# Linear attention into a gated MLP on one core: the first w_in chunk in three loads, batch 2's queries transposed by TensorE, and two block products left whole

## The chip, the cores and the metric

The kernel runs on one core of one Trainium2 chip. The metric is the device time of one execution in microseconds, lower is better. The core has five engines with instruction streams of their own: TensorE (PE in the profile, its weight loads PEld), VectorE (DVE), ScalarE (ACT), GpSimd (POOL) and SyncE (SP). They run side by side and wait for each other through semaphores. SP, ACT and POOL also start DMA transfers.

## The reference

Eight batches of eight heads with 576 rows of 64 values go through an attention without a score matrix; its output, 4608 rows of 512 values, goes through a layer of 2048 units with the activation h * sigmoid(beta * h).

```python
q_s = exp(q - max(q, -1));  q_s = q_s / (sum(q_s, -1) + 1e-09)     # softmax over the 64 values of a row
k_s = exp(k - max(k, 2));   k_s = k_s / (sum(k_s, 2) + 1e-09)      # softmax over the 576 rows
kv  = einsum('bhsd,bhse->bhde', k_s, v)
x   = einsum('bhsd,bhde->bhse', q_s, kv)       # to rows of 512: 8 heads x 64
h   = x @ w_in                                 # 4608 x 512 @ 512 x 2048
g   = h * (1.0 / (1.0 + exp(-beta * h)))
out = g @ w_out                                # 2048 x 512
```

All inputs and the output are float32.

## The kernel before

**Slabs.** The 4608 rows are cut into nine slabs `t` of 512 rows: slabs 0 to 7 are the first 512 rows of batches 0 to 7, slab 8 holds the last 64 rows of all eight batches. A slab has two passes on PE. Pass 1 makes the hidden units: 16 tiles of 128 units, each of four matmuls of 512 columns over the four 128-row blocks `m` of w_in (`pass1_lead` for the first three tiles, block by block; `pass1_tile` for the others; L377). ACT puts each tile through Silu into GT (L623), DVE divides it by beta (L646).

**Pass 2.** From slab 1 on (`pass2_fast`, L712) the second pass forms the product with w_out by seven block products in place of eight, in the manner of Strassen and Winograd: each product is 8 steps `i` of two matmuls of 256 columns, 16 matmuls, 112 in all (L723). Sums of blocks of GT are made by DVE for them: GS1 and GS2 (`g_sum1` L677, `g_sum2` L682, made in parts as the tiles come, the last part for step 7 after the last tile), and the differences `g_diff(0)` and `g_diff(1)` (L689) in place. Sums of blocks of w_out (WSUM, L701) are made once, in slab 0. The first product goes into bank `s`, the second into bank `z5`, the third into `z2`. DVE copies `s` to TS (L792), subtracts `z5` (L795), later `z2` (L801). Before the change the first two products are interleaved: steps 0 to 5 of the first, steps 0 to 5 of the second, steps 6 and 7 of the first, steps 6 and 7 of the second.

**Attention, mixed in.** The attention of batch t + 1 is done while slab t runs. ACT takes exponentials of q and k (EQ, EK; L300). `norm_main` (L324) normalizes EQ for `n` head pairs: a row sum on DVE (L331), a reciprocal on DVE (QI, L332), and a multiplication in place on DVE or POOL as its last argument says (L333). The normalized queries must be transposed to QT, in one of two ways: `t_steps` (L379) has PE transpose four 128x128 blocks for each head pair into a PSUM bank (L375) and ACT or DVE copy them out (L395); `turn` (L480) has the DMA crossbar do it, issued by SP (L484). `norm_turn` is `norm_main` on POOL for two head pairs, followed by `turn`. `kv_steps` (L425) multiplies k and v on PE, with two head pairs to a bank, then a reciprocal (L439) and two masked scalings to KVD (L419) on DVE. `out_step` (L451) is one matmul of 512 columns, KVD with QT, and a copy to XT (L457), which is what pass 1 of the next slab reads.

**The order.** Each engine works through its instructions in the order in which the program adds them. PE's order is set by slots: in each slab, pass 1 takes slots 0 to 64 and pass 2 slots 64 to 128. Each matmul of pass 1 advances the count by 1, each of the 112 of pass 2 by 32/56. A list `todo` of (slot, step) pairs is worked off as the count passes them; `spread(steps, lo, hi)` places steps evenly between two slots. `attn_late(b)` (L509) gives the list for batch b in slabs 1 to 3. Work of the other engines that goes with pass 2 is tied to hooks 0 to 7, points between the products: hook 0 before the first product, 1 and 2 around the first subtraction, 3 after the third product.

**Slab 0.** The loads of w_in and w_out are started by POOL in sequence (`load_win` L545, `load_wout` L551; they cast to bf16). w_in's first chunk of 512 units comes in two parts of two blocks `m` each, the three others whole. Batch 1's q is loaded when w_out's first chunk has landed (L901). Its four head pairs are then normalized one by one and transposed by PE in slots 97, 106, 114 and 119 of slab 0, whose second pass is plain (`pass2_group`, 64 matmuls of 512 columns). Between the normalizations DVE makes the rest of WSUM.

Of the kernel before, what the change touches and what calls it, by code (L numbers as in the profile page):

```python
# [20 lines left out]
NG = NF // 2  # L21
# [133 lines left out]
def bass_efficient_attn_shen__then__act_swish_beta_kernel(  # L155
# [12 lines left out]
    with ExitStack() as es:  # L168
# [340 lines left out]
        def attn_late(b):  # L509
            x = []  # L510
            for hp in range(NHP):
                x += out_step(b, hp, MB, ACTE if hp % 2 else DVE)
            k01, k23 = kv_steps(b, (0, 1)), kv_steps(b, (2, 3))
            if b < 4:
                s = spread(k01, 97, 101) + spread(k23, 101, 105) + [(105, lambda: g_diff(1))]
                return s + spread(x[0:2], 117, 120)
            s = spread(k01, 92, 96) + spread(k23, 96, 99.8) + [(100, lambda: g_diff(1))]
            return s + spread(x, 107, 123)
# [26 lines left out]
        def load_win(c0, c1, m0=0, m1=NM):  # L545
            a = bass.AP(win_h, c0 + 128 * m0 * DFF, [[DFF, 128], [128 * DFF, m1 - m0], [1, c1 - c0]])
            add(POOL, lambda e: e.dma_start(WIN[:, m0:m1, c0:c1], a),  # L547
                w=[("win", f, m) for f in range(c0 // 128, c1 // 128) for m in range(m0, m1)],
                slot=f"win{c0}_{m0}", after=P.writer[("kf", 0, 0)] if c0 == m0 == 0 else ())
# [21 lines left out]
        warm(10, 0)  # L571
        norm_main(0, 0, 1, DVE)
        norm_main(0, 1, 1, POOL)
        load_win(0, 512, 0, 2)
        load_win(0, 512, 2, 4)
        for c0 in range(512, DFF, 512):
            load_win(c0, c0 + 512)
# [134 lines left out]
        def pass2_fast(t, tick, hooks):  # L712
            s, z5, z2 = HB[hrot[0] % 3], OB[0], OB[1]
            z2s = (OB[1], MB[0]) if t == NSLAB - 1 else (z2, z2)

            def prod(bk, lhs, lk, rhs, rk, first, end=False, part=range(NG)):
                two = bk == z2 and z2s[0] != z2s[1]
                for i, u in ([(i, u) for u in range(2) for i in part] if two and end else
                             [(i, u) for i in part for u in range(2)]):
                    l, r_ = lhs(i, u), rhs(i)  # L720
                    st = first and i == 0 and (u == 0 or two)
                    b_ = z2s[u] if two else bk
                    add(PE, lambda e, l=l, r_=r_, st=st, u=u, i=i, b_=b_: e.matmul(  # L723
                        PS[b_][:, 256 * u:256 * u + 256], l, r_, start=st, stop=end and i == NG - 1,
                        skip_group_check=True),
                        r=lk(i) + rk(i), w=[("ps", b_)], bank=[b_])
                    tick(32.0 / 56)

            def gt(f0, th):
                return (lambda i, u: GT[:, f0 + i, 256 * th + 128 * u:256 * th + 128 * u + 128],  # L730
                        lambda i: [("gt", f0 + i, th)])

            def gs2(th):
                return (lambda i, u: GS2[:, i, 256 * th + 128 * u:256 * th + 128 * u + 128],
                        lambda i: [("gs2", i)])

            def wo(fh, dh):
                return (lambda i: WOUT[:, NG * fh + i, 256 * dh:256 * dh + 256],
                        lambda i: [("wout", NG * fh + i, dh)])

            def wsum(n):
                return lambda i: WSUM[n][:, i, :], lambda i: [("ws", n, i)]

            def out(th, dh):
                return (O2S[t % 2][:, 2 * th:2 * th + 2, 256 * dh:256 * dh + 256],
                        [("o2", t % 2, 2 * th + u, dh) for u in range(2)])

            def bank3(bk):
                return PS[bk][:, :].rearrange("p (a b) -> p a b", b=256)

            def halves(bk):
                if bk == z2 and z2s[0] != z2s[1]:
                    return [(z2s[0], 0, 1), (z2s[1], 1, 2)]
                return [(bk, 0, 2)]

            def copy(bk, th, dh, eng):
                o, w = out(th, dh)
                for b_, u0, u1 in halves(bk):
                    add(eng, lambda e, b_=b_, u0=u0, u1=u1: (  # L759
                        e.copy if eng == ACTE else e.tensor_copy)(  # L760
                        o[:, u0:u1, :], bank3(b_)[:, u0:u1, :]),
                        r=[("ps", b_)], w=w[u0:u1], bank=[b_])
                if t == 8:
                    store8(th, dh)

            def last(bk, th, dh):
                o, w = out(th, dh)
                ts = TS[:, :].rearrange("p (a b) -> p a b", b=256)
                h = halves(bk)
                for b_, u0, u1 in h:  # L770
                    add(DVE, lambda e, b_=b_, u0=u0, u1=u1: e.tensor_tensor(  # L771
                        o[:, u0:u1, :], ts[:, u0:u1, :], bank3(b_)[:, u0:u1, :], ALU.add),
                        r=["ts", ("ps", b_)], w=w[u0:u1], bank=[b_])
                    if t == 8 and len(h) == 2:
                        store8(th, dh, u0)
                if t == 8 and len(h) == 1:
                    store8(th, dh)

            def at(n):
                for f in hooks.get(n, ()):  # L780
                    f()

            at(0)
            def prod_s(part):
                prod(s, lambda i, u: GS1[:, i, 128 * u:128 * u + 128], lambda i: [("gs1", i)],
                     *wsum(0), True, True, part)

            prod_s(range(0, 6))
            prod(z5, *gs2(0), *wo(1, 1), True, False, range(0, 6))
            prod_s(range(6, NG))  # L790
            prod(z5, *gs2(0), *wo(1, 1), True, False, range(6, NG))
            add(DVE, lambda e: e.tensor_copy(TS[:, :], PS[s][:, :]), r=[("ps", s)], w=["ts"],  # L792
                bank=[s])
            at(1)
            add(DVE, lambda e: e.tensor_tensor(TS[:, :], TS[:, :], PS[z5][:, :], ALU.subtract),  # L795
                r=["ts", ("ps", z5)], w=["ts"], bank=[z5])
            at(2)
            prod(z2, *gs2(1), *wo(0, 0), True)
            for b_, u0, u1 in halves(z2):
                c = slice(256 * u0, 256 * u1)  # L800
                add(DVE, lambda e, b_=b_, c=c: e.tensor_tensor(  # L801
                    TS[:, c], TS[:, c], PS[b_][:, c], ALU.subtract),
                    r=["ts", ("ps", b_)], w=["ts"], bank=[b_])
            if t > 3:
                g_diff(0)
                g_diff(1)
            at(3)
            prod(z5, *gt(0, 0), *wo(0, 1), False)
            copy(z5, 0, 1, ACTE)
            at(4)  # L810
            prod(z2, *gt(NG, 1), *wo(1, 0), False)
            copy(z2, 1, 0, ACTE)
            at(5)
            prod(z5, *gt(0, 1), *wsum(1), False, True)
            last(z5, 1, 1)
            at(6)
            prod(z2, *gt(NG, 0), *wsum(2), False, True)
            last(z2, 0, 0)
            at(7)
# [12 lines left out]
        def one(fn, *a):  # L832
            return lambda: fn(*a)

        def steps(fn, *a):
            return lambda: go(fn(*a))

        for t in range(NSLAB):
# [12 lines left out]
                todo += [(2, steps(out_step, 0, 3, HEAD, DVE))]  # L851
            elif t < 4:
                todo = attn_late(t + 1)
                if t > 1:
                    todo += [(1, steps(out_step, t, 2, MB, ACTE)), (2.5, steps(out_step, t, 3))]
                if t == 3:
                    todo += [(4, one(norm_turn, 4, 2))]
                if t == 1:
                    todo += [(1, steps(out_step, 1, 2, (3,), ACTE)),
                             (3, steps(kv_steps, 1, (3,), (7,))),  # L860
                             (6, steps(out_step, 1, 3, (7,), DVE)),
                             (6.1, one(w_diff, 0)), (6.2, one(w_diff, 1))]
            elif t < 7:
                todo = attn(t + 1)
                if t > 3:
                    todo += spread(outr_steps(2 * t - 5), *((72, 88), (40, 56), (60, 76))[t - 4])
            elif t == 7:
                todo = spread(outr_steps(1), 32, 48)
# [31 lines left out]
            if t == 0:  # L900
# [6 lines left out]
                w_sum(0, 0, 4)  # L907
                w_sum(2, 0, 4)
                norm_main(1, 0, 1, DVE)
                norm_main(1, 1, 1, DVE)  # L910
                cast_vr_s(1)
                w_sum(0, 4, 4)
                w_sum(2, 4, 4)
# [29 lines left out]
            if t == 1:  # L943
                on(0, exps, 2)
                on(0, casts, 2)
                on(2, norm_turn, 2, 0)
                on(3, norm_turn, 2, 2)
                on(3, g_diff, 0)
                on(3, load, 4)
            elif t == 2:  # L950
                on(0, exps, 3)
                on(2, norm_turn, 3, 0)
# [67 lines left out]
```

## Time and profile before

| what | value |
|---|---|
| time, median of 3 runs | 274.92 us (274.59 to 274.92) |
| profiled execution, its own time | 274.92 us |
| its span | 273.1 us |
| granted clock of TensorE | 0.998 |
| PE, PEld busy | 265.5 us, 167.3 us |
| DVE, ACT, POOL busy | 193.3, 180.7, 62.2 us |
| slab 0: pass 1, pass 2 begin | 14.8, 28.9 us |
| slab 1: pass 1, pass 2 begin | 45.9, 61.1 us |
| slab 2: pass 1, pass 2 begin | 75.1, 89.4 us |
| slab 3: pass 1, pass 2 begin | 103.9, 117.9 us |
| slab 8: pass 2 begins | 257.1 us |

The span is the time from the first to the last instruction that the profile holds; the rest of the execution's own time lies around it. Times in the timeline are counted from the span's start. In a row of the timeline or of a group there stand the start and duration (or the total and mean), the engine, the line of the kernel, the operation, the tiles that it writes and reads with their shapes, and how often it occurs. "[0.63 <-DVE EQ L333]" says how long the engine was idle before, and which instruction released it. Matmul times are modelled: the records of two matmuls overlap, and the distance of their starts is what one takes.

### The profile page before, as it was taken

Reading aid. Unit: us, or ns where it says so; the run is one execution under the profiler, and the core shown is the slowest. Engines: PE = TensorE matmul, PEld = TensorE weight load, DVE = VectorE, ACT = ScalarE, POOL = GpSimd, SP = SyncE. Lnnn points to the kernel's source line nnn. Section 1 sums busy time; section 2 is a strip of 40 time slices with the busy share of each in tenths; the row PEclk is TensorE's granted clock in tenths of the full one; section 3 lists DMA queues with packets and bytes.
Section 4 is the critical chain, followed back from the end, with each engine's and each line's share of the span. In section 5 each row is a group of like instructions: output and inputs, shape, how many; then the busy total and the mean of one; then the engine's idle time right before and its main releaser. Section 6 shows DMA issues by size and latency. Waiting matters only on the chain.

```text
span 273.1 us, 4650 instructions
## 1 busy us (share of the span) xinstructions
PE 265.5 (97%) x1802; PEld 167.3 (61%) x1825; DVE 193.3 (71%) x415; ACT 180.7 (66%) x284; POOL 62.2 (23%) x81
## 2 busy tenths in 40 slices
PE   8899999999999999999999999999999999999994
PEld 2444445448844884478656875587558745874683
DVE  4954586787867799768776976977597549625762
ACT  4898558789287956896778847893783477018610
POOL 2780010006530099000910570037000100000000
PEclk9999999999999999999999999999999999999999
DMA  7999999989599239920499999103600130012005
GB/s 218 316 201 207 226 327 351 293 253 383 119 339 251 100 61 313 340 61 0 96 289 276 352 323 171 77 7 75 209 2 0 22 154 0 2 58 96 2 1 152
DMA packets 59365, 45.92 MB, mean 168 GB/s; under 512 B 28608, under 2 KB 58320, under 8 KB 58320
## 3 DMA queue, kind: packets, MB, share of 16 engines
q1 hardware_dynamic: 54480, 40.90, 52.7%
q0 software_dynamic: 4240, 4.19, 9.3%
q10 hardware_dynamic: 624, 0.53, 0.6%
q8 instruction: 14, 0.23, 0.3%
q14 instruction: 7, 0.06, 0.1%
HBM read 36.71 MB, written 9.44 MB: 169 GB/s over the span
## 4 chain that ended last, share of the span: by engine, by line
PE 80%; DMA 9%; DVE 4%; POOL 4%; issue 1%; ACT 0%; SPq 0%; POOLq 0%; DVEq 0%
PE PS L377 47%; PE PS L723 33%; DMA WOUT<-in_moe_w_out_dram 5%; DMA QF<-in_q_dram 3%; POOL EQ L333 2%; POOL WIN L547 1%; DVE QS L331 1%; DMA QT<-EQ 1%; DVE EQ L333 1%; DVE WSUM L701 0%; DVE QI L332 0%; PE PS L375 0%; DVE XT L457 0%; DVE TS L792 0%; DVE TS L795 0%
## 5 line engine op out<-in xcount | busy, mean ns | idle before, releaser
L377 PE MATMUL PS<-XT,WIN 128*128 128x512 bf16 x562 | 129.6, 379 | 0.8
L623 ACT ACTIVATE GT<-PS,BETA 128x512 bf16<-128x512 f32 x144 | 95.1, 689 | 38.8 <-PE PS L377 38.3
L377 PEld LDWEIGHTS PS<-XT,WIN 128*128 128x128 bf16 x576 | 53.7, 98 | 60.8 <-DVE XT L457 0.6
L646 DVE TENSOR_SCALAR GT<-GT,RB 128x512 bf16<-128x512 bf16 x144 | 51.7, 378 | 36.4 <-ACT GT L623 35.7
L333 POOL TENSOR_TENSOR EQ<-EQ,QI 128x1024 bf16<-128x1024 bf16 (+1 forms) x13 | 25.6, 1967 | 49.9 <-DVE QI L332 49.2
L723 PE MATMUL PS<-WOUT,GT 128*128 128x256 bf16 x256 | 33.9, 273 | 0.1
L723 PE MATMUL PS<-WOUT,GS 128*128 128x256 bf16 x256 | 31.8, 273 | 0.2
L723 PE MATMUL PS<-WSUM,GT 128*128 128x256 bf16 x256 | 30.4, 272 | 0.2
L723 PEld LDWEIGHTS PS<-WSUM,GT 128*128 128x128 bf16 x256 | 24.9, 98 | 4.0 <-issue 0.6
L723 PEld LDWEIGHTS PS<-WOUT,GT 128*128 128x128 bf16 x256 | 24.9, 98 | 3.4
L723 PEld LDWEIGHTS PS<-WOUT,GS 128*128 128x128 bf16 x256 | 24.5, 98 | 3.4
L759 ACT COPY O2S<-PS 128x512 f32<-128x512 f32 (+1 forms) x17 | 9.4, 560 | 25.6 <-PE PS L723 24.2
L300 ACT ACTIVATE EQ<-QF 128x512 bf16<-128x512 f32 x32 | 17.9, 619 | 7.8 <-DMA QF<-in_q_dram 7.7
L682 DVE TENSOR_TENSOR GS<-GT 128x512 bf16<-128x512 bf16 (+2 forms) x32 | 21.9, 685 | 0.0
L377 PE MATMUL PS<-VB,EK 128*128 128x129 bf16 x128 | 20.9, 220 | 0.2 <-DVE VB L348 0.2
L348 POOL CAST VB<-VF 128x512 bf16<-128x512 f32 x25 | 15.4, 617 | 24.1 <-DVE GS L682 14.5
L331 DVE TENSOR_REDUCE QS<-EQ 128x16 f32<-128x1024 bf16 (+1 forms) x20 | 19.8, 991 | 0.6 <-ACT EQ L300 0.6
L689 DVE TENSOR_TENSOR GT<-GT 128x2048 bf16<-128x2048 bf16 x16 | 20.1, 1283 | 0.0
L300 ACT ACTIVATE EK<-KF 128x512 bf16<-128x512 f32 x32 | 18.1, 620 | 0.0
L457 ACT CAST XT<-PS 128x512 bf16<-128x512 f32 x18 | 10.3, 581 | 10.6 <-PE PS L377 10.6
L771 DVE TENSOR_TENSOR O2S<-TS,PS 128x512 f32<-128x512 f32 (+1 forms) x17 | 10.7, 642 | 9.3 <-PE PS L723 9.3
L723 PE MATMUL PS<-WSUM,GS 128*128 128x256 bf16 x128 | 16.7, 273 | 0.0
(78 smaller groups left out, 232.3 us busy)
## 6 DMA issues: line engine op xcount, KB each, us to landing
out_dram<-O2S SPq DMA_DIRECT2D x8, 1024.0 KB, 5.2
QF<-in_q_dram SPq DMA_DIRECT2D x6, 1024.0 KB, 6.0
KF<-in_k_dram SPq DMA_DIRECT2D x6, 1024.0 KB, 8.5
VF<-in_v_dram SPq DMA_DIRECT2D x6, 1024.0 KB, 12.3
KF<-in_k_dram SPq DMA_DIRECT2D x8, 256.0 KB, 5.6
VF<-in_v_dram SPq DMA_DIRECT2D x8, 256.0 KB, 5.6
WOUT<-in_moe_w_out_dram POOLq DMA_DIRECT2D x4, 512.0 KB, 16.6
WIN<-in_moe_w_in_dram POOLq DMA_DIRECT2D x3, 512.0 KB, 9.2
```

Of the source, the lines that this page charges most:

```text
L300: add(ACTE, lambda e, o=o, a=a: e.activation(o, a, ACT.Exp), r=[(name + "f", i, hp)], w=[("e" + name, i, hp)])
L331: add(DVE, lambda e: e.tensor_reduce(s_, a, AX.X, ALU.add), r=ks, w=[("qs", i, hp0)])
L333: add(eng, lambda e: e.tensor_tensor(a, a, vb, ALU.mult), r=ks + [("qi", i, hp0)], w=ks)
L348: add(eng, lambda e: (e.copy if eng == ACTE else e.tensor_copy)(o, a), r=[("vf", i, hp), ("vone", i)], w=[("vb", i, hp)], after=after)
L377: add(PE, lambda e: e.matmul(o, l, r_, start=start, stop=stop), r=r, w=w, bank=[bk])
L457: add(eng, lambda e: (e.copy if eng == ACTE else e.tensor_copy)(XT[i][:, hp, :], PS[bk][:, :]), r=[("ps", bk)], w=[("xt", i, hp)], bank=[bk])
L623: add(ACTE, lambda e: e.activation(GT[:, f, :], PS[bk][:, :], ACT.Silu, scale=BETA[:, f:f + 1]), r=[("ps", bk), "beta"], w=[("gt", f, 0), ...
L646: add(DVE, lambda e: e.tensor_scalar(GT[:, f, :], GT[:, f, :], RB[:, f:f + 1], None, ALU.mult), r=k + ["rb"], w=k)
L682: add(DVE, lambda e: e.tensor_tensor(GS2[:, i:i + n, :], GT[:, i:i + n, :], GT[:, i + NG:i + NG + n, :], ALU.add), r=[k_ for f in (i, i + ...
L689: add(DVE, lambda e: e.tensor_tensor(gv(f, th, NG), gv(f, th, NG), gv(f, 1 - th, NG), ALU.subtract), r=gk(f, 0, NG) + gk(f, 1, NG), w=gk(f ...
L723: add(PE, lambda e, l=l, r_=r_, st=st, u=u, i=i, b_=b_: e.matmul(PS[b_][:, 256 * u:256 * u + 256], l, r_, start=st, stop=end and i == NG - ...
L771: add(DVE, lambda e, b_=b_, u0=u0, u1=u1: e.tensor_tensor(o[:, u0:u1, :], ts[:, u0:u1, :], bank3(b_)[:, u0:u1, :], ALU.add), r=["ts", ("ps ...
```

## The change

There are five edits.

- w_in's first chunk loads in three parts: block 0, block 1, then blocks 2 and 3.
- In slab 0 the multiplication for head pair 1 of batch 1 goes from DVE to POOL.
- In slab 1, batch 2's queries are transposed by PE in place of the crossbar: `norm_turn` gives way to `norm_main` on POOL, and `t_steps` for head pairs 0 and 1 and for 2 and 3 come into PE's order in slots 104 to 107 and 116.5 to 119. The KV products move from 97 to 105 to 107 to 113, `g_diff(1)` from 105 to 113.5, the first two output steps from 117 to 120 to 114 to 116. The last two output steps move from the start of slab 2 to slots 123 to 126 of slab 1.
- The loads of batch 4 are issued at hook 0 of slab 1 in place of hook 3.
- In every `pass2_fast` the first product is done whole, then the second whole.

```diff
--- before.py
+++ after.py
@@ -511,7 +511,12 @@
             for hp in range(NHP):
                 x += out_step(b, hp, MB, ACTE if hp % 2 else DVE)
             k01, k23 = kv_steps(b, (0, 1)), kv_steps(b, (2, 3))
-            if b < 4:
+            if b == 2:
+                s = spread(t_steps(b, (0, 1), MB, ACTE), 104, 107) + spread(k01, 107, 110)
+                s += spread(k23, 110, 113) + [(113.5, lambda: g_diff(1))] + spread(x[0:2], 114, 116)
+                s += spread(t_steps(b, (2, 3), MB, ACTE), 116.5, 119)
+                return s + spread(x[2:4], 123, 126)
+            if b == 3:
                 s = spread(k01, 97, 101) + spread(k23, 101, 105) + [(105, lambda: g_diff(1))]
                 return s + spread(x[0:2], 117, 120)
             s = spread(k01, 92, 96) + spread(k23, 96, 99.8) + [(100, lambda: g_diff(1))]
@@ -571,7 +576,8 @@
         warm(10, 0)
         norm_main(0, 0, 1, DVE)
         norm_main(0, 1, 1, POOL)
-        load_win(0, 512, 0, 2)
+        load_win(0, 512, 0, 1)
+        load_win(0, 512, 1, 2)
         load_win(0, 512, 2, 4)
         for c0 in range(512, DFF, 512):
             load_win(c0, c0 + 512)
@@ -713,10 +719,10 @@
             s, z5, z2 = HB[hrot[0] % 3], OB[0], OB[1]
             z2s = (OB[1], MB[0]) if t == NSLAB - 1 else (z2, z2)
 
-            def prod(bk, lhs, lk, rhs, rk, first, end=False, part=range(NG)):
+            def prod(bk, lhs, lk, rhs, rk, first, end=False):
                 two = bk == z2 and z2s[0] != z2s[1]
-                for i, u in ([(i, u) for u in range(2) for i in part] if two and end else
-                             [(i, u) for i in part for u in range(2)]):
+                for i, u in ([(i, u) for u in range(2) for i in range(NG)] if two and end else
+                             [(i, u) for i in range(NG) for u in range(2)]):
                     l, r_ = lhs(i, u), rhs(i)
                     st = first and i == 0 and (u == 0 or two)
                     b_ = z2s[u] if two else bk
@@ -781,14 +787,9 @@
                     f()
 
             at(0)
-            def prod_s(part):
-                prod(s, lambda i, u: GS1[:, i, 128 * u:128 * u + 128], lambda i: [("gs1", i)],
-                     *wsum(0), True, True, part)
-
-            prod_s(range(0, 6))
-            prod(z5, *gs2(0), *wo(1, 1), True, False, range(0, 6))
-            prod_s(range(6, NG))
-            prod(z5, *gs2(0), *wo(1, 1), True, False, range(6, NG))
+            prod(s, lambda i, u: GS1[:, i, 128 * u:128 * u + 128], lambda i: [("gs1", i)],
+                 *wsum(0), True, True)
+            prod(z5, *gs2(0), *wo(1, 1), True)
             add(DVE, lambda e: e.tensor_copy(TS[:, :], PS[s][:, :]), r=[("ps", s)], w=["ts"],
                 bank=[s])
             at(1)
@@ -851,10 +852,9 @@
                 todo += [(2, steps(out_step, 0, 3, HEAD, DVE))]
             elif t < 4:
                 todo = attn_late(t + 1)
-                if t > 1:
-                    todo += [(1, steps(out_step, t, 2, MB, ACTE)), (2.5, steps(out_step, t, 3))]
                 if t == 3:
-                    todo += [(4, one(norm_turn, 4, 2))]
+                    todo += [(1, steps(out_step, 3, 2, MB, ACTE)), (2.5, steps(out_step, 3, 3)),
+                             (4, one(norm_turn, 4, 2))]
                 if t == 1:
                     todo += [(1, steps(out_step, 1, 2, (3,), ACTE)),
                              (3, steps(kv_steps, 1, (3,), (7,))),
@@ -907,7 +907,7 @@
                 w_sum(0, 0, 4)
                 w_sum(2, 0, 4)
                 norm_main(1, 0, 1, DVE)
-                norm_main(1, 1, 1, DVE)
+                norm_main(1, 1, 1, POOL)
                 cast_vr_s(1)
                 w_sum(0, 4, 4)
                 w_sum(2, 4, 4)
@@ -943,10 +943,10 @@
             if t == 1:
                 on(0, exps, 2)
                 on(0, casts, 2)
-                on(2, norm_turn, 2, 0)
-                on(3, norm_turn, 2, 2)
+                on(0, load, 4)
+                on(2, norm_main, 2, 0, 2, POOL)
+                on(3, norm_main, 2, 2, 2, POOL)
                 on(3, g_diff, 0)
-                on(3, load, 4)
             elif t == 2:
                 on(0, exps, 3)
                 on(2, norm_turn, 3, 0)
```

## The prediction

> **What bounds the kernel.** I read the page first: the shares of busy time, then the waits of the engines, then the timeline around each edited place.
>
> ```profile
> PE 265.5 (97%) x1802; PEld 167.3 (61%) x1825; DVE 193.3 (71%) x415; ACT 180.7 (66%) x284; POOL 62.2 (23%) x81
> ```
>
> TensorE is busy for 97% of the span, so work added to PE or a new wait of PE goes to the end nearly one for one, and work taken off another engine pays only where PE waited. The windows by stage say where that is: slab 7's second pass, with nothing mixed in, takes 12.2 us for its 112 products, 0.109 each; slab 1's takes 14.0 us (61.09 to 75.11), of which 13.7 are 112 x 0.109, twenty 0.056 us KV products and two of 0.216. From slab 3 on I find no PE hole that isn't a whole number of products, which I take for lost records (1802 matmuls stand against 1825 weight loads).
>
> Where PE does wait for other engines, in the list of waits (all of PE, one line of the weight loads):
>
> ```profile
> PE PS L375 <- DVE EQ L333: 1.0, 2, 0.6
> PEld PS L377 <- DMA QT<-EQ: 0.9, 3, 0.5
> ```
>
> A weight load may sit early without PE losing time, so I price from matmul starts: in slab 1 the crossbar's landings cost PE 0.02 us (75.34), the subtraction on GT 0.06, EKR 0.16 (68.13). In slab 2 they cost 0.09, 0.13 and 0.28, the last at 103.89.
>
> **The w_in load, in three.** A start of a w_in load holds POOL for 0.73 to 0.95 us (median 0.81). But from 15 us on the queue drains by bytes: the landings of the two 256 KB parts are 1.34 us apart, of 512 KB parts 2.52. One more start then costs 2 x 1.34 - 2.52 = 0.16 us in the queue. PE starts the first block at 14.80 and was held there by the attention's KVD, not by w_in, so an earlier first block brings nothing. The next chunk lands at 18.47 and PE has 0.06 us of slack there; w_out's first chunk lands at 27.13 and releases batch 1's q load, the chain that PE waits for at 40.96. Both move together: +0.16. Bounds 0 (all hidden by the backlog) and 0.81 (the start comes out in full); I take 0.16, since every later start is issued by 17 us and lands up to 20 us later. The Trainium skill's page "DMA: Bandwidth & Descriptors" (Anatomy of one DMA) gives every such DMA some 2.0 us fixed; were these in series, the total would be 1.8 us more, but the 1.34 us row is less than that for a whole part.
>
> **norm_main(1, 1) from DVE to POOL.** DVE now:
>
> ```profile
> 37.20 0.20 DVE L332 RECIPROCAL QI<-QS 128x8 f32<-128x8 f32 x1
> 37.44 0.69 DVE L333 TENSOR_TENSOR EQ<-EQ,QI 128x512 bf16<-128x512 bf16 x1
> 38.05 1.29 DVE L701 TENSOR_TENSOR WSUM<-WOUT 128x1024 bf16<-128x1024 bf16 x2
> 39.25 0.68 DVE L331 TENSOR_REDUCE QS<-EQ 128x8 f32<-128x512 bf16 x1
> ```
>
> and PE transposes head pair 1 at 38.21 without waiting, head pair 2 at 40.96 after a wait of 0.63. POOL does the same multiplication in 1.04 (its only 512-wide one), starting at about 37.56: done 38.60, PE starts at 38.65, 0.44 late. DVE runs 0.6 ahead, head pair 2 is ready at 40.3, and PE, after 4 transposes (0.22) and 8 products (1.73), gets there at 40.6: 0.36 gained, and 0.05 more at head pair 3. That is one end, -0.41. The other comes from what POOL suffers beside DVE's two-input bf16 work, which the WSUM sums are:
>
> ```profile
> 67.39 4.74 POOL L333 TENSOR_TENSOR EQ<-EQ,QI 128x1024 bf16<-128x1024 bf16 x2
> 69.12 1.26 DVE L689 TENSOR_TENSOR GT<-GT 128x2048 bf16<-128x2048 bf16 x1
> 71.74 1.48 DVE L689 TENSOR_TENSOR GT<-GT 128x2048 bf16<-128x2048 bf16 x1
> ```
>
> Of the 4.74, the first multiplication is 1.90, as it is everywhere else; the second, begun at 69.38 beside the first subtraction (to 70.37), is 2.76: 0.86 longer, nearly all of the overlap. So I let POOL stand still while such a sum runs. Behind one WSUM (to 38.0) it ends at 39.0, the second WSUM waits in turn, and PE does head pair 2 at 41.2: +0.25. Behind both it ends at 39.65 and PE gets to head pair 2 at 41.6: +0.62. I take +0.40, between these two. The skill's page "SBUF — State Buffer" (Who interferes with whom) calls this an exclusive lock held for the whole instruction, whoever comes first; by that rule -0.41 is impossible and only +0.25 or +0.62 is left.
>
> **Batch 2's queries on PE.** Added to slab 1's second pass: 16 transposes. Four take from 38.21 to 38.44, 0.056 each: 0.89 us on PE. The two evictions of 128x1024 bf16 go to ACT, about 1.0 each (512-wide: 0.58). Gone: the two crossbar transfers, with the waits of slab 1 above, 0.02 + 0.06 + 0.16 (KV comes 10 slots later, after EKR): -0.24. The two output products of head pairs 2 and 3 only move from the start of slab 2 to the end of slab 1: 0.
>
> New waits. The first transposes are due at slot 104, after 70 products: 61.09 + 70 x 0.109 + 0.14 (next part) = 68.87. POOL's first multiplication starts only when the four V casts end (67.29) and ends at 69.29; PE goes on at 69.35: 0.48. Behind it in PE's order stand all remaining products, so nothing fills it. Then the KV products end 10 slots later: the last starts at about 72.6. DVE's reciprocal follows after 0.26, two KVD 0.6 later, and only then g_diff(1), at 73.6, which takes 1.22 alone; PE resumes 0.15 after a g_diff ends (73.22 to 73.36 now): 74.97. PE would want it after 96 products, at 74.64: 0.33. The second eviction, begun 0.22 after the last transpose, ends as PE reaches output step 2: 0.05. Sum: 0.89 - 0.24 + 0.48 + 0.33 + 0.05 = +1.51. Floor 0.65 (no new wait); ceiling 2.2 (g_diff(1) at its contended 1.48, POOL 0.4 later).
>
> load(4) goes to SP ahead of where the crossbar transfers were; behind its waits for the exponentials stands only store(1). It is issued by about 68 in place of 73.4 to 81: nobody waits for either, 0. If it did collide it would meet store(0), which lands at 71.4 and is waited for by no one in that pass.
>
> **The first two products whole.** Slab 1 now:
>
> ```profile
> 61.09 1.47 PE L723 MATMUL PS<-WSUM,GS 128*128 128x256 bf16 x12
> 62.40 0.29 DVE L677 TENSOR_TENSOR GS<-GT 128x256 bf16<-128x256 bf16 x1
> 62.40 1.47 PE L723 MATMUL PS<-WOUT,GS 128*128 128x256 bf16 x12
> ```
>
> GS1's last block is written at 62.69, 1.60 after the pass begins, in every slab. Whole, the first product wants it as its 15th matmul: 61.09 + 14 x 0.109 = 62.62. A released weight load starts 0.05 after its producer's end, so PE goes at 62.75: 0.13, with the restart 0.14. This recurs in slabs 1 to 8; in slab 6 three or four remainder products of 0.03 come before it and leave 0.03. Slab 1 (0.14), slabs 3, 4, 5, 7, 8 (5 x 0.14) and slab 6: 0.87. GS2's last block (1.94 after the start) is wanted after 3.3: hidden.
>
> In return the copy of the first bank starts at 2.1 in place of 3.26 after the pass begins, and the first subtraction, which then waits for the second product, at 3.83 in place of 4.05. Only slab 2 has a PE wait behind that chain (norm, POOL, crossbar): of its 0.50, 0.36 goes (0.22 from the chain, 0.14 because PE itself is later). Its own stall is 0.14, net -0.22.
>
> **The sum.** 0.16 + 0.40 + 1.51 + 0.87 - 0.22 = +2.72. The profiled execution took 274.92 (273.1 of span and 1.8 around it), which is the median too, so 277.6.
>
> **Rivals.**
> Not slower: DVE's queue in the first slab is worth far more than I say. In the list of waits the weight loads of the transposes wait 3.0 us for DVE's EQ, six times. If the 0.69 taken off DVE came back at each of the four steps between 38 and 46, 2.8 us would be gained in place of my -0.40, and the total would be 2.72 - 0.40 - 2.8 = -0.5: 274.4. It decides at 38.2: POOL must be done by then, in 0.65 us. The 1.04 of its row and DVE's strict order (one relief shifts everything once) speak against it; for it, only that weight loads do wait. Chance 0.06.
> The small waits don't show: GS1 is in time and POOL doesn't hold up slot 104. Then transposes, the queue and POOL's head pair 1 are left: 0.16 + 0.40 + 0.65 - 0.36 = +0.85: 275.8. Against it, the release rows; a matmul that leaves 0.1 later hides all of it. Chance 0.19.
> The extra start reaches the q chain in full, 0.81, and POOL stands behind both sums: 0.65 + 0.22 more: 278.5. For it: POOL's starts are strictly in series; against it, the backlog. Chance 0.15.
> My forecast: 0.60.
>
> **The numbers.** 277.6; the range from 275.9, just above the second rival, to 278.7, past the third. 0.2%, about what a measurement of this kernel can tell from no change, is 0.55 us. The first rival is split between faster (0.05) and same; with the small end of the second, same gets 0.04; slower 0.91.
>
> **What would show it.** The profile after should have: a wait of PE for DVE's GS (L677) of about 0.13 near the 15th product of each second pass but slab 6's; L375 with 16 more matmuls, one wait for POOL's EQ near 69 and one for DVE's GT (L689) near 75; slab 1's second pass about 16.1 us long; a POOL multiplication of over 1.04 near 37.6 and head pair 1 about 1 us late; slab 2 losing most of its wait at 103.9. I am wrong if slabs 3 to 8 keep their length, or if head pair 1 isn't late.

## Result and the profile after

The changed kernel takes 277.28 us (median of 6 runs, 276.96 to 277.73) against 274.92 (6 runs, 274.59 to 275.83): the ratio is 1.0083, 95% interval 1.0067 to 1.0099. It is slower by 2.36 us; 277.6 was predicted. The profiled execution took 277.27 us, of which 275.2 are its span. Lines have moved: by 5 or 6 between the first edits and the product order (L677 is now L683, L689 is L695, L723 is L729), by 1 behind it (L792 is L793).

The busy times of the page after:

```profile
PE 267.3 (97%) x1818; PEld 167.6 (61%) x1841; DVE 194.1 (71%) x414; ACT 183.0 (66%) x286; POOL 63.4 (23%) x83
```

PE has 16 instructions more and is still busy for 97%: the loss is the 16 transposes and many short waits, and the stages say where. The windows by stage, first before and then after, each row from one start of a pass to another; columns are the window, its length, the busy time (instructions) of PE, PEld, DVE, ACT and POOL, the granted clock, the share of the DMA engines and GB/s:

```profile
28.93:45.89 16.96, 16.22 (x96) 7.88 (x97) 12.21 (x27) 10.42 (x19) 1.22 (x2) 1.00 1.14 305
61.09:75.11 14.02, 13.97 (x135) 12.11 (x134) 11.33 (x22) 8.54 (x15) 8.32 (x8) 1.00 0.84 254
257.05:269.28 12.23, 12.23 (x113) 10.86 (x111) 7.06 (x13) 1.95 (x5) 0.00 (x0) 1.00 0.17 44
```

```profile
28.98:46.17 17.19, 16.41 (x97) 7.79 (x97) 12.31 (x26) 10.53 (x19) 2.53 (x3) 1.00 1.13 304
61.36:77.46 16.10, 15.77 (x153) 13.08 (x153) 12.15 (x23) 11.01 (x18) 8.35 (x8) 1.00 1.07 364
259.15:271.52 12.37, 12.37 (x113) 10.78 (x111) 7.06 (x13) 1.95 (x5) 0.00 (x0) 1.00 0.17 42
```

Slab 0's second pass is 0.23 longer, slab 1's 2.08 (of which 0.43 are the two output products that came from slab 2), slab 8's 0.14. From start to start of the second passes, so that this move cancels:

| stage | after minus before, us | predicted |
|---|---|---|
| slab 0, to slab 1's first pass | +0.28 | +0.56 |
| slab 1, from there to slab 2's second pass | +1.61 | +1.65 |
| slab 2's second pass and slab 3's first | -0.37 | -0.22 |
| the same for slabs 3, 4, 5, 6, 7 | +0.14, +0.13, +0.14, +0.03, +0.14 | 0.14 each, 0.03 in 6 |
| slab 8's second pass | +0.14 | +0.14 |

That is 2.24 at the last matmul; the two profiled executions differ by 2.35. Two rows need care. Slab 1 begins at 45.78 to 46.01 in the four profiles whose slab 0 is that of the kernel before, and at 46.02 to 46.44 in the three with both of slab 0's edits, so the +0.28 is good to some 0.2. And the slab 2 row compares with 28.55 in the kernel before, while seven other profiles with its product order have 28.33 to 28.42: against those the row would be -0.16 to -0.24. The rows of slabs 3, 5, 6 and 7 are the same to 0.01 in every profile with the same product order.

The weight loads' waits after name the new ones:

```profile
PEld PS L375 <- POOL EQ L333: 2.2, 3, 1.2
PEld PS L729 <- DVE GS L683: 1.7, 7, 0.2
```

Seven waits for GS1's last block are slabs 1 to 5, 7 and 8; the one in slab 6, of 0.13, is too short for the list, and the line on the crossbar's QT is gone. A weight load stands idle for 0.25 there, while the matmuls lose 0.13. The weight loads of PE and the rows of DVE in slab 1:

```profile
63.02 0.11 PEld L729 LDWEIGHTS PS<-WSUM,GS 128*128 128x128 bf16 x2 [0.25 <-DVE GS L683]
```

```profile
62.67 0.29 DVE L683 TENSOR_TENSOR GS<-GT 128x256 bf16<-128x256 bf16 x1
63.45 0.69 DVE L793 COPY TS<-PS 128x512 f32<-128x512 f32 x1 [0.15 <-PE PS L729]
```

The block is written at 62.96, 1.60 after the pass begins at 61.36; the load goes 0.06 later. The copy comes 2.09 after the pass begins, as forecast.

### The profile page after: what moved, and what is told of

Read it like the earlier page. It is cut to its first block, busy times and chain, and to the rows that moved or that the text cites. A ratio compares the mean times of both kernels' runs of the same rounds, so it can differ in the third digit from the quotient of the medians.

```text
span 275.2 us, 4686 instructions
## 1 busy us (share of the span) xinstructions
PE 267.3 (97%) x1818; PEld 167.6 (61%) x1841; DVE 194.1 (71%) x414; ACT 183.0 (66%) x286; POOL 63.4 (23%) x83
## 4 chain that ended last, share of the span: by engine, by line
PE 82%; DMA 8%; POOL 4%; DVE 2%; issue 1%; ACT 0%; SPq 0%; POOLq 0%
PE PS L377 48%; PE PS L729 33%; DMA WOUT<-in_moe_w_out_dram 5%; DMA QF<-in_q_dram 3%; POOL EQ L333 2%; POOL WIN L552 2%; PE PS L375 1%; POOL VB L348 1%; DVE QS L331 1%; POOL VR L362 0%; DVE XT L457 0%; ACT GT L629 0%; DVE EQ L333 0%; DVE QI L332 0%; ACT EQ L300 0%
## 5 line engine op out<-in xcount | busy, mean ns | idle before, releaser
L652 DVE TENSOR_SCALAR GT<-GT,RB 128x512 bf16<-128x512 bf16 x144 | 52.3, 383 | 36.7 <-ACT GT L629 35.9
L333 POOL TENSOR_TENSOR EQ<-EQ,QI 128x1024 bf16<-128x1024 bf16 (+1 forms) x14 | 26.6, 1898 | 67.3 <-DVE QI L332 66.3
L729 PE MATMUL PS<-WOUT,GT 128*128 128x256 bf16 x256 | 33.6, 273 | 0.1
L729 PE MATMUL PS<-WSUM,GT 128*128 128x256 bf16 x256 | 31.9, 272 | 0.2
L729 PE MATMUL PS<-WOUT,GS 128*128 128x256 bf16 x256 | 30.4, 273 | 0.2
L729 PEld LDWEIGHTS PS<-WSUM,GT 128*128 128x128 bf16 x256 | 24.9, 98 | 4.0 <-issue 0.2
L729 PEld LDWEIGHTS PS<-WOUT,GT 128*128 128x128 bf16 x256 | 25.0, 98 | 3.4
L729 PEld LDWEIGHTS PS<-WOUT,GS 128*128 128x128 bf16 x256 | 24.6, 98 | 3.4
L695 DVE TENSOR_TENSOR GT<-GT 128x2048 bf16<-128x2048 bf16 x16 | 19.8, 1263 | 0.0
L729 PE MATMUL PS<-WSUM,GS 128*128 128x256 bf16 x128 | 16.4, 273 | 0.0
```

What stands on the lines that cost most here:

```text
L333: add(eng, lambda e: e.tensor_tensor(a, a, vb, ALU.mult), r=ks + [("qi", i, hp0)], w=ks)
L652: add(DVE, lambda e: e.tensor_scalar(GT[:, f, :], GT[:, f, :], RB[:, f:f + 1], None, ALU.mult), r=k + ["rb"], w=k)
L695: add(DVE, lambda e: e.tensor_tensor(gv(f, th, NG), gv(f, th, NG), gv(f, 1 - th, NG), ALU.subtract), r=gk(f, 0, NG) + gk(f, 1, NG), w=gk(f ...
```

## Experiments

**The four parts, each alone on the kernel before.** The kernel before took 274.98 beside them.

*w_in's first chunk in three loads:*

```diff
-        load_win(0, 512, 0, 2)
+        load_win(0, 512, 0, 1)
+        load_win(0, 512, 1, 2)
```

> Only the three-part load of w_in's first chunk, on the kernel before. Theory (the queue drains by bytes, one more start costs it 0.16 us): w_out's first chunk lands at about 27.30 in place of 27.13, batch 1's q chain and PE's wait near 41 move by 0.16, slab 1 begins 0.2 us later and nothing else changes: 275.1. Rival (a start's 0.8 us on GpSimd comes out in full): 27.9 and 275.7. Second rival (PE gains from an earlier first block): slab 0 begins before 14.8 and the time is below 274.9.

275.15 us, ratio 1.0001 (0.9988 to 1.0015): not to be told from nothing. Slab 0 begins at 14.66 in place of 14.80, but in this profile the first load was started 0.28 earlier as well, and the time isn't lower, so the second rival falls. Slab 1 begins at 46.02 in place of 45.89. w_out's first chunk lands 17.85 after the first start; in the nine profiles with the load in two parts that runs from 17.49 to 17.73, with one of 17.97, and in the four with three parts from 17.64 to 18.25. The 0.8 in full is ruled out; 0.16 lies inside the scatter.

*Head pair 1 on POOL:*

```diff
-                norm_main(1, 1, 1, DVE)
+                norm_main(1, 1, 1, POOL)
```

> Only head pair 1's multiplication of batch 1 goes from DVE to POOL. Theory (POOL and a two-input DVE sum stop each other; POOL waits for the rest of the first WSUM, the second WSUM waits for POOL): the POOL row takes 1.3 in place of 1.04, the second WSUM 1.5 in place of 0.68, PE starts head pair 1 about 0.7 late and head pair 2 within 0.1 to 0.25 of where it was: 275.0. Rival (freeing DVE of 0.69 pays): head pair 2 is 0.4 or more earlier, 274.5 or less.

275.03, ratio 0.9998 (0.9984 to 1.0013). The timeline of this run, POOL and then DVE:

```profile
37.56 1.31 POOL L333 TENSOR_TENSOR EQ<-EQ,QI 128x512 bf16<-128x512 bf16 x1 [17.16 <-DVE QI L332]
```

```profile
37.33 2.09 DVE L701 TENSOR_TENSOR WSUM<-WOUT 128x1024 bf16<-128x1024 bf16 x2
39.34 0.67 DVE L331 TENSOR_REDUCE QS<-EQ 128x8 f32<-128x512 bf16 x1
```

POOL takes 1.31 in place of 1.04, the two sums 2.09 in place of 1.29, and head pair 2's row sum comes at 39.34 in place of 39.25: all of DVE's relief is gone. PE starts head pair 1 at 38.92 (before: 38.21), head pair 2 at 41.03 (before: 40.96; 40.85 to 41.07 in three other profiles with an unchanged slab 0, so the 0.07 is inside the scatter). The rival, which had head pair 2 come 0.4 earlier, falls.

*The first two products whole:*

```diff
-            prod_s(range(0, 6))
-            prod(z5, *gs2(0), *wo(1, 1), True, False, range(0, 6))
-            prod_s(range(6, NG))
-            prod(z5, *gs2(0), *wo(1, 1), True, False, range(6, NG))
+            prod(s, ..., True, True)
+            prod(z5, *gs2(0), *wo(1, 1), True)
```

> Only the first two block products left whole. Theory (PE waits 0.13 for GS1's last block in each second pass, 0.03 in slab 6; slab 2 gets its wait for the crossbar back): slabs 3 to 8 are 0.72 longer together, slab 2 0.3 to 0.4 shorter, slab 1 0.0 to 0.14 longer: 275.3. Rival (the earlier copy and subtraction free DVE and later waits take the 0.13 back in every slab): 274.6.

275.50, ratio 1.0018 (1.0002 to 1.0034). The seven waits for GS are there (1.7 us in all, as above); the stage from slab 2's second pass is 0.37 shorter, slab 1 unchanged, slab 3 0.14 longer, slab 7 and slab 8 0.14 each. Slab 4's stage is 0.36 longer; 0.22 of that is a wait in slab 5's first pass for the crossbar's remainder queries (QTR), where a weight load stands idle for 0.5 in place of 0.2; such a wait shows in runs without this edit too (0.6 with head pair 1 on POOL alone). The rival, which had the 0.13 paid back in every slab, falls.

*Batch 2's queries on PE:* the edits of `attn_late`, of slab 1's hooks and of the output steps, as in the change.

> Only batch 2's queries on PE, with the moved KV products, output steps and loads. Theory: 0.89 of transposes, a wait of 0.6 for POOL's multiplication near slot 104 (0.14 more than with the whole products, which come 0.14 later there), 0.33 for the second subtraction on GT, 0.15 at an output step, less 0.24 of waits that go: slab 1's second pass 1.7 longer (beyond the 0.43 of two output products that move into it), nothing later: 276.6. Rival (only the transposes' own work counts, the waits are filled): 0.65, 275.6.

276.48, ratio 1.0053 (1.0038 to 1.0067). This is the largest part. Slab 1's second pass takes 16.12, and PE waits 0.51 before the first transpose (0.35 in the changed kernel, where PE comes 0.13 later). The four medians give 0.17 + 0.05 + 0.52 + 1.50 = 2.24 of the 2.36; the four ratios give 1.93. The parts add as far as their intervals, of some 0.4 us each way, can tell.

**Two of the new waits taken away from the changed kernel.** The kernel before took 275.06 beside these.

*Step 7 of the first product put off:*

```diff
-            prod(s, ..., True, True)
-            prod(z5, *gs2(0), *wo(1, 1), True)
+            prod_s(range(0, 7))
+            prod(z5, *gs2(0), *wo(1, 1), True, False, range(0, 2))
+            prod_s(range(7, NG))
+            prod(z5, *gs2(0), *wo(1, 1), True, False, range(2, NG))
```

> The changed kernel, with one step of its product order put back: steps 0 to 6 of the first product, 0 and 1 of the second, 7 of the first, 2 to 7 of the second. Step 7 of the first then comes 0.44 later, after GS1's last block. Theory (the 0.13 is the wait for that block and nothing else of the order): no wait for GS1 in any second pass; slabs 3, 4, 5, 7 and 8 are 0.14 shorter each, slab 2 0.14 shorter and still without its waits for the crossbar; slab 1 unchanged, because the wait for POOL near slot 104 grows by the same 0.14: 276.4 against the changed kernel's 277.28. Rival (the whole order itself costs, through the bank or the weight loads): 277 or more.

276.44, ratio to the kernel before 1.0049 (1.0036 to 1.0063), so 0.84 less than the changed kernel. No wait for GS is left. Slab 3's stage is back at 29.17 and slab 8's second pass at 12.23, and the wait for POOL grows to 0.49, as it had to. The 0.13 is the wait for that block and nothing else of the order.

*KV products ahead of the first transposes:*

```diff
-                s = spread(t_steps(b, (0, 1), MB, ACTE), 104, 107) + spread(k01, 107, 110)
+                s = spread(k01, 104, 107) + spread(t_steps(b, (0, 1), MB, ACTE), 107, 110)
```

> The changed kernel with the first eight transposes of batch 2 (slots 104 to 107) and the ten KV products after them (107 to 110) exchanged. Theory (PE waits 0.46 there for POOL, which is held up by its V casts): the KV products need nothing of POOL's second piece of work, PE gets to the transposes about 1.1 later and waits for nothing; the wait for the second subtraction on GT stays at 0.25: slab 1's second pass 15.65 in place of 16.1, 276.8. Rival (the wait only moves, to the subtraction or to the eviction of the queries before the first output step): 277.2 to 277.4.

276.96, ratio 1.0069 (1.0055 to 1.0083), 0.32 less than the changed kernel. Slab 1's second pass is 15.74 in place of 16.10, PE goes into the transposes without a wait, and the waits behind stay as they were (0.25 for the second subtraction, 0.15 at an output step). The wait doesn't move on; 0.1 less is gained than I expected, since the wait had been 0.35 and not 0.46.

**DVE's queue in slab 0.** In the prediction PE's wait of 0.63 near 41 came from two WSUM sums ahead of head pair 2's row sum.

*The sums in slab 1:*

```diff
-                w_sum(0, 4, 4)
-                w_sum(2, 4, 4)
...
+                             (6.05, one(w_sum, 0, 4, 4)), (6.06, one(w_sum, 2, 4, 4)),
                              (6.1, one(w_diff, 0)), (6.2, one(w_diff, 1))]
```

> The kernel before, with the two WSUM sums that stand between head pairs 1 and 2 of batch 1 on DVE moved to slab 1, just ahead of the differences of w_out. Theory (PE's 0.63 near 41 is DVE's queue: the sums come before head pair 2's row sum): head pair 2's EQ is ready at 39.7, PE doesn't wait near 41, slab 1 begins 0.65 earlier; DVE is 1.3 later with slab 1's first tiles and has caught up before GS1: 274.3. Rival (q's landings set the pace, or DVE is missed in slab 1): 274.8 or more.

274.71, ratio 0.9989 (0.998 to 0.9998). Slab 1 begins at 45.30, 0.59 earlier, as the theory has it. But the profile gives it back in slab 1's second pass, which takes 14.82. PE and the rows of SP there:

```profile
73.02 0.49 PE L723 MATMUL PS<-WSUM,GT 128*128 128x256 bf16 x3 [0.90 <-DMA QT<-EQ]
```

```profile
68.72 4.07 SPq L484 DMA_TRANSPOSE QT<-EQ  x2
```

The first crossbar transfer lands at 72.75, 4.03 after its issue (3.15 in the kernel before), 0.89 behind slab 0's store, which lands at 71.86. The store was under way in the kernel before too, but landed 2.04 after the transfer's issue; here it lands 3.14 after. In the run with the whole products alone it landed 2.34 after, and the transfer, again 0.89 behind it, took 3.23. So the rows fit a transfer that lands no sooner than some 0.9 behind the store; that the store is the cause is argued from them, not shown by a run. I had priced the crossbar's landing at nearly nothing; here it is on the path. The profiled execution took 275.19, the second slowest of twelve (274.27 to 275.21), so this wait need not be in all of them.

*The same with head pair 1 on POOL:* both edits.

> The same with head pair 1's multiplication on POOL besides. Theory (POOL's 1.31 in place of 1.04, and the second WSUM's 1.53 in place of 0.68, were the two stopping each other): with no two-input DVE sum beside it POOL takes 1.04, PE starts head pair 1 0.45 late and doesn't wait after that; slab 1 begins 0.4 earlier than in the kernel before, 0.25 later than with the sums moved alone: 274.55. Rival (POOL's 1.31 is its own, from a colder start after 17 us of rest): 1.31 again, PE 0.7 late, 274.8.

274.62, ratio 0.9986 (0.9976 to 0.9996).

```profile
37.53 1.04 POOL L333 TENSOR_TENSOR EQ<-EQ,QI 128x512 bf16<-128x512 bf16 x1 [17.14 <-DVE QI L332]
```

With no two-input sum beside it POOL takes 1.04 after the same rest of 17 us: the 0.27 was the neighbour, not a cold start. PE starts head pair 1 at 38.63 and slab 1 at 45.51, 0.38 earlier than in the kernel before (0.41 was the good end of my bounds). Here the crossbar landed in time.

**Toward a faster kernel.** The kernel before took 275.01 beside these.

*The kernel before with step 7 put off:* steps 0 to 5 and 6 to 7 become 0 to 6 and 7, with two steps of the second product between, as above.

> The kernel before, with one edit to the product order: steps 0 to 6 of the first product, 0 and 1 of the second, 7 of the first, 2 to 7 of the second. Theory (the whole products' gain in slab 2 is the earlier subtraction, and it can be had without the wait for GS1): no wait for GS1 in any second pass, slab 2's second pass 0.4 to 0.5 shorter as with the whole products, slab 1 up to 0.1 shorter, the other slabs unchanged: 274.5. Rival (the gain in slab 2 needs the first product to be done as early as in the whole order): 274.9.

274.71, ratio 0.9983 (0.9969 to 0.9997). Slab 2's second pass and slab 3's first are 0.5 shorter (28.04 in place of 28.55, or 0.3 to 0.4 against the seven other profiles named above), no wait for GS appears. The interleaving needs one step, not two, to cover the block, and the early subtraction is worth 0.3 to 0.4 in slab 2, about what the time shows.

*The sums in slab 1, slab 0's store behind the crossbar transfers:*

```diff
-                    if n == 10:
-                        store(0)
...
+                on(3, store, 0)
                 on(3, load, 4)
```

> The two WSUM sums in slab 1 as in the earlier run, and slab 0's store issued behind batch 2's two crossbar transfers, in place of ahead of them. Theory (with the sums moved alone, slab 1's gain of 0.6 was lost because the first crossbar transfer had the store's data in front of it in the DMA queue and landed 4.0 after its issue in place of 3.15): it lands 3.1 after its issue, PE's wait of 0.85 at the first output step shrinks to under 0.1, and the 0.6 of slab 0 stays: 274.3. Rival (the transfer is slow for another reason, and an earlier slab 1 always meets it): 274.7 as before.

274.60, ratio 0.998 (0.997 to 0.999). The transfer is issued at 69.10 and lands at 72.24, 3.14 later, and slab 1's second pass is 14.02 again. But slab 0's gain shrank to 0.2, for the reason that the next run shows, so the transfer was issued 0.38 later than with the sums moved alone. That leaves the store untested: with head pair 1 on POOL besides, the store did stand ahead, the transfer was issued at 68.94, and it took 3.14 all the same.

*All of it,* with slab 5's remainder products in slots 44 to 60 in place of 40 to 56:

> The kernel before, with what the runs point to: the product order with step 7 put off, the two WSUM sums in slab 1, slab 0's store behind the crossbar transfers, and the remainder products of slab 5 four slots later (44 to 60), since their crossbar transfer lands within 0.3 of its use there. Theory (each part takes away a wait of PE of its own): 0.6 in slab 0, 0.4 to 0.5 in slab 2, up to 0.2 in slab 5: 273.8. Rival (the parts meet the same next wait, the crossbar's landings in slabs 1 and 2): 274.3 or more.

274.06 us, ratio 0.9961 (0.9946 to 0.9977): faster than both kernels, by 0.4% and 1.2%, if not by as much as hoped. In slab 0 of the profiled execution (274.38) PE now waits for the first V cast on POOL. POOL, PE and DVE of this run:

```profile
40.94 0.99 POOL L348 CAST VB<-VF 128x512 bf16<-128x512 f32 x1 [0.57 <-DMA VF<-in_v_dram]
```

```profile
41.98 0.40 PE L377 MATMUL PS<-VB,EK 128*128 128x129 bf16 x4 [0.56 <-POOL VB L348]
```

```profile
40.76 0.69 DVE L333 TENSOR_TENSOR EQ<-EQ,QI 128x512 bf16<-128x512 bf16 x1
```

and the same moment in the run with the sums moved alone:

```profile
40.74 0.61 POOL L348 CAST VB<-VF 128x512 bf16<-128x512 f32 x1 [0.38 <-DMA VF<-in_v_dram]
```

```profile
40.75 1.14 DVE L333 TENSOR_TENSOR EQ<-EQ,QI 128x512 bf16<-128x512 bf16 x1
```

Where DVE starts first, POOL's cast takes 0.99 and PE waits; where POOL starts first by 0.02, it takes 0.61, DVE 1.14, and PE doesn't. The V load landed at 40.88 and 40.68, while DVE started within 0.01 of the same time: 0.2 in a landing decides it here.

*w_in's first chunk in four loads:* `for m in range(4): load_win(0, 512, m, m + 1)` in place of the two loads.

> The kernel before, with w_in's first chunk in four loads of one block. Theory (each further start costs the queue a fixed amount, about 0.16): w_out's first chunk lands 0.3 later than in the kernel before relative to the first start, slab 1 begins 0.3 later: 275.3. Rival (what the three-part load cost is scatter of the profile): landing and slab 1 within 0.1 of the kernel before, 275.0.

275.03, ratio 0.9997 (0.9984 to 1.001). PE begins slab 0 at 14.46 and takes 14.84 for its first pass in place of 14.13, since the second chunk lands later (18.88); slab 1 begins at 45.88 as before, and w_out's first chunk lands 17.74 after the first start. So neither an earlier first block nor a later second chunk reaches the end: the q chain decides, and two more starts don't delay it measurably. The price per start is not borne out.

## Why the prediction was right

The waits that it named are there, at their places. Its sum, +2.72, was 0.36 too high against the times and 0.48 at the last matmul: there 0.28 in slab 0, 0.15 in slab 2, the rest small. These errors have the same sign, so the total owes nothing to errors that cancel.

**Whole products.** Right to 0.01: 0.14 in each of slabs 3, 4, 5, 7 and 8 and 0.03 in slab 6, with the place (the 15th product), the producer and the time of its end read from the profile of before. The run with step 7 put off shows that this is the cause.

**Batch 2 on PE.** 1.61 of 1.65. The rows of the changed kernel that hold PE up:

```profile
67.65 4.74 POOL L333 TENSOR_TENSOR EQ<-EQ,QI 128x1024 bf16<-128x1024 bf16 x2
69.60 0.28 PE L375 MATMUL PS<-IDB,EQ 128*128 128x128 bf16 x2 [0.19 <-POOL EQ L333]
73.77 1.22 DVE L695 TENSOR_TENSOR GT<-GT 128x2048 bf16<-128x2048 bf16 x1
75.07 1.01 ACT L395 COPY QT<-PS 128x1024 bf16<-128x1024 bf16 x1 [0.59 <-PE PS L375]
75.13 1.03 PE L729 MATMUL PS<-WSUM,GT 128*128 128x256 bf16 x8
76.14 0.39 PE L377 MATMUL PS<-QT,KVD 128*128 128x512 bf16 x1
```

POOL's first multiplication ends at 69.55, DVE's subtraction at 74.98, ACT's copy at 76.09; each time PE goes on 0.05 to 0.15 later. The wait for POOL was 0.35 (0.459 between two matmul starts, 69.14 to 69.60, less the 0.109 that one takes; forecast 0.48), for the second subtraction 0.25 (0.33), at the output step 0.15 (0.05), and one of 0.07 before the last transposes was not foreseen. The transposes themselves are the larger half, and nothing on PE could hide them.

**Slab 2.** The mechanism held: DVE's chain there came 0.22 sooner (the first subtraction starts 3.83 after the pass begins in place of 4.05), as forecast. The 0.14 of the waits that the sum let stay went too: the crossbar transfer at the chain's end took 3.17 (102.13 to 105.30) in place of 3.39 (100.45 to 103.85), 0.22 less. That isn't the change's doing, since this transfer takes 3.14 to 3.26 in all profiles but that of the kernel before. Against the seven others with its order the gain is 0.16 to 0.24, around the forecast 0.22, so part of the -0.37 is chance.

**Head pair 1 on POOL.** The step that was mis-sized: +0.40, between POOL waiting for one sum and for both, against 0.07 to 0.08 measured, within the scatter of slab 0. It was the first case, POOL behind one sum, and even that (+0.25) was dear: the first sum ends at 37.97, as priced, but POOL is done at 38.87 in place of 39.0, and the second sum at 39.42, 0.55 behind it and not 0.68. The rule of the page "SBUF — State Buffer" (Who interferes with whom), an exclusive lock for a whole instruction to whoever comes first, fits every row here to within some 0.15: POOL's 0.27 behind a sum, the sum's 0.85 behind POOL (1.53 in place of 0.68), and both orders of the V cast. It was the better guide than my "stands still", which doesn't say who goes first.

**The third load.** Its +0.16 can't be confirmed: the profile after has w_out's first chunk 0.17 later, but the part alone and the four loads don't show it apart from scatter. The term was worked out from a 512 KB load cut into two, where the edit cuts one of 256 KB: the profile after has the two 128 KB parts land at 13.95 and 14.58 and the next 256 KB 1.34 later, and the same sum from these is 2 x 0.63 - 1.34 = -0.08, no price. The fixed 2.0 us for each such DMA that "DMA: Bandwidth & Descriptors" (Anatomy of one DMA) states is paid beside the others here, as landings 0.63 apart show; in the run with four loads two more starts moved the landing by less than 0.3.

**The rivals.** The one that ended at 274.4 is refuted by the POOL row of 1.31; the small waits did show (against the second); the extra start did not come out in full (against the third).

## What to carry to other kernels

Where one engine is busy for 97%, price an edit from that engine's own order: count what is added to it, and for each operand it now wants sooner compare the writer's end with the moment it arrives; here that gave 0.14 us in five slabs to a hundredth. Work moved between DVE and POOL to relieve one of them is worth only what is left after they have blocked each other, so look first at what stands beside it; moving the two sums out of the way did what moving the multiplication could not. A transfer that costs nothing today may only be landing just in time: the gain of an earlier stage can end at it.

## What the runs showed that was not expected

- Slab 1's first crossbar transfer took 3.13 to 3.23 us from issue to landing in nine profiles and 4.03 in the one where slab 0's store landed 3.14 after its issue, with slab 1 begun 0.6 earlier; there it sat on the path.
- The crossbar transfer of the remainder queries in slab 5 lands within 0.3 of its use: PE lost 0 to 0.30 there in different profiles (0.30 in the run with head pair 1 on POOL alone), which alone makes kernels that agree everywhere else differ by 0.1%.
- A difference of some 0.2 us between a load's landing and DVE's start turns over which of DVE and POOL goes first, and moves slab 1 by 0.4 (45.30 and 45.68 in two kernels that differ only behind it; there the load landed 0.05 later and DVE started 0.14 sooner).
